# Batch 0 of k as fp32 over two hardware queues with a cast on chip, and a newly searched fixed order of all instructions

## Chip, cores, metric

One core of one Trainium2 chip. The metric is device time in microseconds (us) of one execution. Times are medians; comparisons use the runs in the fast state, taken on the same chip in the same rounds, with a 95% interval. A run counts as slow when it is over 1.5% above the fastest run of the same kernel.

## The reference, cut

```python
def phi(x):                                   # w_phi: 64 x 128
    proj = np.einsum('bhsd,df->bhsf', x, w_phi)
    proj = proj - np.max(np.abs(proj), axis=-1, keepdims=True)
    return np.concatenate([np.exp(proj), np.exp(-proj)], axis=-1)
q_p, k_p = phi(q), phi(k)                     # q, k, v: 8 x 8 x 576 x 64, fp32
kv  = np.einsum('bhsf,bhsd->bhfd', k_p, v)
num = np.einsum('bhsf,bhfd->bhsd', q_p, kv)
den = np.einsum('bhsf,bhf->bhs', q_p, np.sum(k_p, axis=2))[..., None] + 1e-06
x = (num / den)                               # then heads side by side: 4608 x 512
h = x @ w_in                                  # 512 x 2048
g = np.where(h > 0, h, np.exp(np.minimum(h, 0)) - 1)
out = g @ w_out                               # 2048 x 512
```

## The kernel before

The kernel is one long list of steps. One letter is one step of one kind, taken in turn from that kind's list of pieces; a star sends the step to the other of two engines, and a digit names a PSUM bank. Each engine executes its own instructions in the order in which the list has them. So the string below is the schedule.

```python
ORDER = """
eacdbeefgj7kfA0gj7BekBA2A4fCBj7hl6Bkl1hmBmA6gCBM0BCj3DBkENA4Dl3BEOmBP2l1EQCS2m*CFA0FTM6ECU4DTUNE
...                                           # 24 such lines
"""
for letter, star, bank in re.findall(r"([A-Za-z])(\*?)(\d?)", "".join(ORDER.split())):
    fn, args = queues[letter]
    ...
    fn(*next(args), **how)
```

The letters that matter here are: a start (w_phi, identity), b cast of w_phi, e/f/g loads of k/q/v, h/i loads of w_in/w_out, j/k transposes of k on TensorE and their copy, n/o DMA transposes of k and q, A k times w_phi, C its maximum, E v times its scale, S q times w_phi, x/R/y the division of the attention's result, z DMA transposes of that result into xT, p x @ w_in, q/r/s the ELU, t @ w_out. The prediction calls some steps by name: h_mm is p, q_mm S, m_mm M, x_mm W, v_scale E, h_elu s, x_scale y; kv_copy (V) and o_copy (u) copy products out of PSUM, the memory that TensorE writes to. Of the tiles, w_sb is the cast w_phi, mk the maxima of C, vs v times its scale em, and denj the denominator that R forms.

```python
def start():
    w_f32 = epool.tile([P, CHUNK], FP32, name="e_sb")[:, 0:F]
    for par in range(2):
        queue = (nc.sync, nc.scalar)[par]
        queue.dma_start(out=w_f32[par * D:(par + 1) * D, :], in_=w_phi)
    ...

def load(name, b, p0, p1):                    # e, f, g: fp32 in HBM, bf16 in SBUF
    nat = get((name, b), lambda: io.tile([P, H // 2, NS, D], BF16, name=name + "n"))
    nc.gpsimd.dma_start(out=nat[:, p0:p1]..., in_=src[b]...[:, p0:p1])

def v_scale(n, pr, sg):                       # E
    nc.gpsimd.tensor_tensor(get(("vs", n), new_vs)[:, sg, r, 0:D],
        st["v", n // 2][:, 2 * (n % 2) + pr],
        st["em", n][:, sg, r].unsqueeze(2).to_broadcast((P, NS, D)), op=ALU.mult)

def x_rec(n, part):                           # R: two inputs in SBUF (e1 and xs)
    den = small.tile([P, 7], FP32, name="denj")[:, 0:v1 - v0]
    nc.vector.scalar_tensor_tensor(
        den, st["e1", n][:, 0, v0:v1], 1e-6, st["xs", n, part][:, :, D],
        op0=ALU.mult, op1=ALU.add)
    nc.vector.reciprocal(st["rec", n, part], den)

def x_dma(n, pr, mixed):                      # z: xp (bf16) -> xT, read by h_mm (p)
    nc.sync.dma_start_transpose(out=xT_of(b)[:, ct]..., in_=xp...)
```

Of the kernel before, what the change touches and what calls it, by code (L numbers as in the profile page):

```python
# [10 lines left out]
FP32 = mybir.dt.float32  # L11
BF16 = mybir.dt.bfloat16
# [31 lines left out]


# [1 line left out]
def kernel(  # L47
# [26 lines left out]
    NS = S // D  # L74
# [10 lines left out]
    io = ctx.enter_context(tc.tile_pool(name="io", bufs=2))  # L85
# [4 lines left out]
    moep = ctx.enter_context(tc.tile_pool(name="moep", bufs=2))  # L90
# [115 lines left out]
    def load(name, b, p0, p1):  # L206
        src = {"k": k, "q": q, "v": v}[name]
        nat = get((name, b), lambda: io.tile([P, H // 2, NS, D], BF16, name=name + "n"))
        nc.gpsimd.dma_start(
            out=nat[:, p0:p1].rearrange("p r s d -> p r (s d)"),  # L210
            in_=src[b]
            .rearrange("h s d -> (h s d)")
            .rearrange("(pr q x) -> q pr x", q=P, x=NS * D)[:, p0:p1],
        )

    def load_w_in(j):
# [6 lines left out]
    def copy_on(scalar):  # L223
        return nc.scalar.copy if scalar else nc.vector.tensor_copy
# [504 lines left out]
    def blocks(name, n):  # L729
        cut = 3 if (name, n) == ("k", 0) else 5  # L730
        return [(name, n, 0, cut), (name, n, cut, NI)]
# [83 lines left out]
```

## Time and profile before

| | before |
|---|---|
| time, median of the three runs | 367.6 us (366.73 to 371.62) |
| span of the profiled run | 365.3 us |
| idle of TensorE between 60 and 361 us | 1.3 us of 301 |

TensorE is full from about 60 us on, and its clock is 0.9 or more of full speed in each of the page's 40 slices.

In the timeline a line is start, duration, queue or engine, source line, operation and operands. In this kernel xT lands 4.2 us after its issue.

### The profile page before, as it was taken

The numbers are of one execution on the slowest core, as the hardware profiler recorded it, in microseconds if no ns is written. First come the engines' busy times: TensorE is split into PE (matmuls) and PEld (weight loads), VectorE is DVE, ScalarE is ACT, GpSimd is POOL, SyncE is SP. The second block draws the span as 40 slices with busy tenths as digits, with TensorE's granted clock in tenths as the row PEclk, the third lists the DMA queues.
The fourth block names the chain that finished last, engine by engine and source line by source line (L and its number), as shares of the span: only waits on it lengthen the run. The fifth ranks groups of instructions, "written<-read, shape, count | busy, mean of one in ns | idle before, by whom it ended". The sixth has DMA issues, their size and how long they took to land.

```text
span 365.3 us, 9809 instructions
## 1 busy us (share of the span) xinstructions
PE 347.5 (95%) x3914; PEld 188.5 (52%) x3914; DVE 269.6 (74%) x476; ACT 251.8 (69%) x479; POOL 213.2 (58%) x323
## 2 busy tenths in 40 slices
PE   3788899999999999999999999999999999999994
PEld 2566676655465454545455445544555444444442
DVE  4899986878876889798978899899858814744300
ACT  4879788877897689877976886888577304554220
POOL 8673848277934988485776597556557404543200
PEclk9999999999999999999999999999999999999999
DMA  7999969599796999866989399053220330214143
GB/s 106 195 213 208 208 100 148 65 166 151 114 144 95 166 171 144 152 89 92 193 162 126 44 173 135 4 110 79 44 48 16 32 75 2 58 29 92 26 99 74
DMA packets 68478, 39.70 MB, mean 109 GB/s; under 512 B 48336, under 2 KB 62800, under 8 KB 68432
## 3 DMA queue, kind: packets, MB, share of 16 engines
q1 hardware_dynamic: 52416, 20.56, 33.1%
q0 software_dynamic: 15856, 18.35, 32.7%
q8 instruction: 30, 0.49, 0.6%
q14 instruction: 16, 0.13, 0.1%
q10 hardware_dynamic: 160, 0.16, 0.1%
HBM read 36.77 MB, written 9.44 MB: 126 GB/s over the span
## 4 chain that ended last, share of the span: by engine, by line
PE 77%; DVE 12%; DMA 7%; issue 1%; POOL 1%; ACT 0%; DVEq 0%; ACTq 0%; POOLq 0%
PE banks L693 32%; PE banks L665 29%; PE banks L509 4%; DMA kT<-kn 3%; DVE mk L305 3%; PE banks L542 3%; PE banks L469 2%; PE banks L287 2%; DVE gT L685 2%; DMA kn<-in_k_dram 2%; DMA qn<-in_q_dram 2%; PE banks L558 2%; DVE mq L388 2%; PE banks L346 2%; DVE xp L575 1%
## 5 line engine op out<-in xcount | busy, mean ns | idle before, releaser
L681 POOL TENSOR_SCALAR e_sb<-e_sb 128x512 f32<-128x512 f32 (+1 forms) x160 | 91.1, 574 | 96.2 <-ACT e_sb L676 93.1
L693 PE MATMUL banks<-w_out_sb,gT 128*128 128x512 bf16 x576 | 138.3, 380 | 0.0
L676 ACT ACTIVATE e_sb<-banks 128x512 f32<-128x512 f32 (+1 forms) x160 | 88.1, 561 | 62.1 <-PE banks L665 57.9
L685 DVE SCALAR_TENSOR_TENSOR gT<-e_sb,banks 128x512 bf16<-128x512 f32 (+1 forms) x160 | 97.0, 626 | 44.9 <-POOL e_sb L681 44.5
L665 PE MATMUL banks<-xT,w_in_sb 128*128 128x512 bf16 (+1 forms) x576 | 123.0, 356 | 1.1 <-DVE gT L685 0.3
L665 PEld LDWEIGHTS <-w_in_sb 128*128 128x128 bf16 x640 | 59.1, 98 | 58.9 <-issue 2.6
L298 ACT ACTIVATE EK<-banks 128x768 bf16<-128x768 f32 x96 | 75.7, 814 | 16.5 <-PE banks L287 14.5
L324 POOL TENSOR_TENSOR vs<-vn,em 128x576 bf16<-128x576 bf16 x64 | 73.6, 1159 | 17.8 <-ACT em L315 17.7
L693 PEld LDWEIGHTS <-gT 128*128 128x128 bf16 x576 | 52.3, 98 | 59.7 <-issue 1.9
L493 ACT ACTIVATE Eq<-banks 128x768 bf16<-128x768 f32 (+2 forms) x96 | 73.5, 813 | 6.9 <-PE banks L481 3.3
L305 DVE TENSOR_REDUCE mk<-banks 128x6 f32<-128x768 f32 x48 | 45.2, 950 | 6.2 <-ACT EK L298 3.9
L374 DVE TENSOR_REDUCE mx<-banks 128x6 f32<-128x768 f32 (+1 forms) x30 | 30.7, 1038 | 4.8 <-PE banks L346 3.8
L608 POOL TENSOR_TENSOR xj<-xs,recj 128x448 bf16<-128x448 f32 (+1 forms) x22 | 20.1, 916 | 13.9 <-DVE recj L603 10.6
L587 DVE TENSOR_TENSOR xs<-banks,e 128x455 f32<-128x455 f32 (+1 forms) x30 | 18.0, 602 | 7.4 <-PE banks L542 5.9
L703 ACT COPY o_sb<-banks 128x512 f32<-128x512 f32 x23 | 13.3, 589 | 14.5 <-PE banks L693 14.5
L509 PE MATMUL banks<-vs,EK 64*128 64x65 bf16 x1152 | 22.9, 192 | 0.2 <-DVE xp L575 0.2
L509 PEld LDWEIGHTS <-EK 64*128 64x128 bf16 x1152 | 20.9, 96 | 2.9 <-issue 1.3
L542 PEld LDWEIGHTS <-Eq 128*128 128x128 bf16 x400 | 16.2, 97 | 7.3 <-issue 1.3
L592 DVE TENSOR_TENSOR xs<-banks,xs 128x455 f32<-128x455 f32 (+1 forms) x30 | 18.3, 610 | 1.1
L287 PE MATMUL banks<-w_sb,kT 64*128 64x128 bf16 x288 | 17.1, 228 | 1.9 <-DVE kT L240 1.1
L542 PE MATMUL banks<-kv_sb,Eq 128*128 128x65 bf16 x400 | 17.2, 193 | 0.5 <-DVE kv_sb L519 0.5
L469 PE MATMUL banks<-qT,w_sb 64*128 64x384 bf16 (+2 forms) x102 | 16.4, 324 | 0.5 <-DVE gT L685 0.2
(66 smaller groups left out, 243.3 us busy)
## 6 DMA issues: line engine op xcount, KB each, us to landing
out_dram<-o_sb SPq DMA_DIRECT2D x71, 128.0 KB, 2.4
kn<-in_k_dram POOLq DMA_DIRECT2D x7, 576.0 KB, 9.2
qn<-in_q_dram POOLq DMA_DIRECT2D x7, 576.0 KB, 7.3
vn<-in_v_dram POOLq DMA_DIRECT2D x7, 576.0 KB, 8.6
w_in_sb<-in_moe_w_in_dram POOLq DMA_DIRECT2D x2, 1024.0 KB, 20.4
w_out_sb<-in_moe_w_out_dram POOLq DMA_DIRECT2D x1, 2048.0 KB, 20.4
qn<-in_q_dram POOLq DMA_DIRECT2D x2, 288.0 KB, 7.4
vn<-in_v_dram POOLq DMA_DIRECT2D x2, 288.0 KB, 8.1
```

The source lines that it names most:

```text
L298: nc.scalar.activation(EK[:, sg, 6 * c:6 * c + 6, :].rearrange("p (i r) f -> p r i f", r=2), st["pk", n, c], ACT.Exp, scale=1.0 - 2.0 * sg,)
L305: nc.vector.tensor_reduce(mk[:, 6 * c:6 * c + 6].rearrange("p (i r) -> p r i", r=2), st["pk", n, c], axis=AX.X, op=ALU.max, apply_absolute ...
L324: nc.gpsimd.tensor_tensor(get(("vs", n), new_vs)[:, sg, r, 0:D], st["v", n // 2][:, 2 * (n % 2) + pr], st["em", n][:, sg, r].unsqueeze(2). ...
L374: nc.vector.tensor_reduce(mq.rearrange("p (v r) -> p r v", r=2)[:, :, v0:v1], st["pm", n, c][:, :, 0:v1 - v0, :], axis=AX.X, op=ALU.max, a ...
L493: nc.scalar.activation(Eq[:, sg, :, :, p0 * D:p1 * D].rearrange("p h r x -> p r h x"), st["pq", n, c][:, :, 0:(p1 - p0) * P].rearrange("p ...
L509: nc.tensor.matmul(kv[:, hi, pr, sg, :], EK[rows, sg, pr * NS + s, :], vs[rows, sg, pr * NS + s, :], start=(s == 0), stop=(s == NS - 1),)
L542: nc.tensor.matmul(pn[:, sg, v - v0, :], Eq[:, sg, hi, par, i0 * D:(i0 + 2) * D], kv_sb[:, hi, pr, sg, :], start=True, stop=True,)
L665: nc.tensor.matmul(ph, w_in_sb[:, ct, jt * P:(jt + 1) * P], xT_of(ch)[:, ct, h0:h1], start=(ct == 0), stop=(ct == N_CT - 1),)
L676: nc.scalar.activation(e_sb, st["ph", ch, jt, h0], ACT.Exp)
L681: nc.gpsimd.tensor_scalar(e_sb, e_sb, 1.0, 0.0, op0=ALU.min, op1=ALU.max)
L685: nc.vector.scalar_tensor_tensor(gT[:, jt, h0:h1], st["e", ch, jt, h0], -1.0, st["ph", ch, jt, h0], op0=ALU.add, op1=ALU.max,)
L693: nc.tensor.matmul(po, st["gT", ch][:, jt, tt * P:(tt + 1) * P], w_out_sb[:, jt, :], start=(jt == 0), stop=(jt == N_JT - 1),)
```

## The change

The intent is to free the software queue (GpSimd's, over which all casting loads go) at the start: k of batch 0 comes as plain fp32 over SyncE's and ScalarE's queues, in four transfers of 288 KB, and VectorE casts it. v_scale may now go to VectorE, and the whole list was searched again with these freedoms. The counts of letters change little (14 of 64 v_scale to VectorE, four kv_copy to ScalarE, three o_copy and two x_scale to VectorE); the matmuls are the same 3914.

```diff
 ORDER = """
-eacdbeefgj7kfA0gj7BekBA2A4fCBj7hl6Bkl1hmBmA6gCBM0BCj3DBkENA4Dl3BEOmBP2l1EQCS2m*CFA0FTM6ECU4DTUNE
-...
+acdGj3kbA0BBfgfGj7kGA6A2GgefBBBCj5j1kA4BBBhhCkl0mCDDl0mA2BA0BBBCM6NOP5Q*l6l7m*CDS2TTCDmFFEEEEE*
+...                                          (24 lines, all new)
     def start():
+        k_f32 = moep.tile([P, H // 2, NS * D], FP32, name="gT")
+        nc.sync.dma_start(out=k_f32[:, 0], in_=k_src[:, 0])
         for par in range(2):
-            queue = (nc.sync, nc.scalar)[par]
-            queue.dma_start(out=w_f32[par * D:(par + 1) * D, :], in_=w_phi)
+            nc.scalar.dma_start(out=w_f32[par * D:(par + 1) * D, :], in_=w_phi)
+        nc.sync.dma_start(out=k_f32[:, 1], in_=k_src[:, 1])
+        nc.scalar.dma_start(out=k_f32[:, 2], in_=k_src[:, 2])
+        nc.sync.dma_start(out=k_f32[:, 3], in_=k_src[:, 3])
+    def k_cast(pr, other=False):              # G, on VectorE
+        copy_on(other)(nat[:, pr]..., st["k_f32"][:, pr])
-    def v_scale(n, pr, sg):
-        nc.gpsimd.tensor_tensor(
+    def v_scale(n, pr, sg, other=False):      # E* is VectorE
+        (nc.vector if other else nc.gpsimd).tensor_tensor(
-        e=(load, [("k", 0, 0, 1), ("k", 0, 1, 2), ("k", 0, 2, 4)]
-           + [("k", *x) for x in all_batches[1:]]),
+        e=(load, [("k", *x) for x in all_batches[1:]]),
+        G=(k_cast, [(pr,) for pr in range(H // 2)]),
```

More of the change, by code (lines that the diff above doesn't have):

```diff
@@ L18 @@
 ORDER = """
-eacdbeefgj7kfA0gj7BekBA2A4fCBj7hl6Bkl1hmBmA6gCBM0BCj3DBkENA4Dl3BEOmBP2l1EQCS2m*CFA0FTM6ECU4DTUNE
-BM2EOVDBNFW6EP5M0XM2Q*S4ENTU6FNOj1iP0UQ*kTS2VM0TNW4TY7OXS0j6Tl3kTY2mP5l4Z*W0mQ*Z*S3XA5Tp7j2qkTS0
-rCp2TM3TsNqp7BrA0sj4qCp3Brp2qsl6BkresM4qmp7BrNp3qM0qsrA4Drsp6Esp2qNl7Bp3rqp1O*sqrY0mrCZ*W6FEsp0B
-XP2gqp5Drp4qQqsrS6srqM2sFTsEM0NTp5rNqp7rS2qsM0sTrY6ENU4TsA0O*A2BUZp7VBp6qP5CBt4rsBS0p7TCtqQ*rW2T
-sp5DnXqW0qrtrXfp6ES2qsA0stBnrFsTp7Eu*t6TCp5qp4rDzqp3sqrp2Brszp7sqp5qrqS0rstrTsoFsEqp4Tp7rqzS2sA0
@@ L24 @@
-rTtEsCToU4qA2BUrzstV*CBW4up7XW0qBt6rXzDBM4FtNzM0M2sA4NvBp7tNqBzrA0sM2O*BCftBENP7t5uQCEDS2M6TtNFe
-TS0M6ETtNTEU2S0A6UTCop4VtqTp3rzBsW0qnp4Xrp2qszW0rqu*O*p3DXvBEp5qsvrp7qrszp6rqsFsA0rqM2np4NBEp5qC
-rzP3p2rQ*sqp3srqsDp7rqsfp6sqrBp5rsqEsM0qA2p4NBrt7BrsqFS0CgtTsrTS2EM5TNS0toTsTA5U2CTUBS0VvtBW2zTt
-6XTW4uzA0DXS2BtETzCtFETtzBA2M4BS0t7oTCtDTNFtEBvM0A4EM2NBtzNeBU0fu*UA2Cp6Bp5Cqut4rDBsEp7qM2V*rp6N
-qEDnW0wstwrqxgM2trNW0FnetxEp5vusS0qM2Rp7syTNp6TFrqS2Rp4qsrTrsp5qsTp7rqysW0qS2xp6rTzrTp4sEzsqA0U2
-qCroUrsBp7RV*syA5BCW2p4zxDqW0Eqxp3Brp2rBsRqA0S5qCnt7rTgRtsvTrstBEvsDS3M5TytNzTt2yu*BW3EzS5xA0tBF
@@ L30 @@
-zTRM3CtyTNFtzBEwM5S0vU3NTUToA5Vt7BuA0CtCzDtBEW2BtfxBA4p6BRyp3CqDEW0u*wp2qxrBp7FqFsrS0M4TEt6NTtrs
-qtRrsM0ysM3p5NEzp7qNp2rzqsW0rqp4nxrp5qevstrsqsrS0uU2RTUy*S6TzVp4TsW0vqp3xTrp5qoRrsA0qS6p2CTrp4Ts
-vqsW6qp3rzBrsp5qexBt2rqRS0DA6srotBsytBsyTA3CtETCzW5Dt7FxFBEtBnRM0yA5M3NBztEutNBzEM0wU2CvfUNDS4V*
-Et6uW0TvW2xTtxA4M0BntRBW2Nyzp7ECtqt1xFDrup5FsEA2qM6p4NBrp0ECqU6srBUqM2V*tNrA5sS2Bp7swRp4TRCyqp0T
-rztqsBtzrqgy*S2u*W5Torp7xDTp1sqS2qRvW5rsTp4rsTp0zyxqW2Fqp7zrsrsA5qvp1gRBxrp4qsBp3rsqyp2Cqrwzt7sq
-rsS0EM5sTtnNTrtEDzsS0M3A5TEtCoTt2NFBEA0U3BCURM5Dty*BEVztBNEW3zu*A0S5xBtTt7CTW3RDtxBEA5wM0Bu*FS3y
@@ L36 @@
-tNBEtTCp2TFuW0qU3xM5rURM0NV*p7yNp4zqsrS5qA0p3sTroCp2Tqsp7qrW4qrsp6DrsBnp3Rqsp2qrvxBt7rzqsA0S4srB
-tsBp6y*TCzp3qRp2qrvwtrsqzsDtrTEsvM0A3M5NBp2ENp1qBru*p0qEsvt7qCFrM5p2rsW3NqtrstFsExA0S5BtyTCt4TRW
-2By*txzDA0U5BRS2zUyBtEV*zCtuFDEvW0TS5xt7TEzTtu*ETS0U2TFS4UwTtVW0p6xp3qRTRW0rtqyTp2rxp5qsp4rqRW0r
-sqp6sursp3yqsp7qrzxp5rqy*zp4qrssW0rzqt6Rrsp3zxp7qy*W0rsqp2xrp5qstrsqtRrsp4systqzRp7rzst5qtrvsty*
-tzt7ztvttt4ttp3p2qp1rqstrqsp3rsp2qt1rqsp0rsp3qtrqsp2rsp0qu*p3rqvstrqsup6rvsp5qp3rqsp2rqsp6rqstrq
-st5rsp3p6qp2rqstrqsp3rsp6qutrqvsp7rsp3qp6rqstrqsup7rvst4qutrvstup7vp6qtrqst5rsp7u*p6qvtrqstrstt7
@@ L42 @@
-p6p4qtrqsp3rstqtrsp6t4qutruvstvtt7utvttt6tutvtt7u*tvttuv
+acdGj3kbA0BBfgfGj7kGA6A2GgefBBBCj5j1kA4BBBhhCkl0mCDDl0mA2BA0BBBCM6NOP5Q*l6l7m*CDS2TTCDmFFEEEEE*
+M4U6NOUM0NV*W6XP4Q*S2TTM0M4NNEEFFU6EUV*OP0QS2TTM0NW5XY4S0TTj7j3j2kkkY5Z*ZgiOP6Q*W0XS3TTA5l2mCS0T
+TM3Nl2mA0CBBp7qp3qrrl4msBj5kp2qp4srM6NBqrsp5qrssY1DZ*M6NA2Bp4qp5p1qqrrrCDsssW6Xp0p4Bqqp5ql1m*p2
+p3p6FFrrrsqqrsp7qsqY4M0sO*P5Q*Z*p2qrrrsssS5TTNM3M0NNp7qS3TTEEE*ErU5sA0CfrsUV*A2p6BBO*P4p7p5eQ*S0
+ot4tqqrrqTTCBrsssBDW6XzEW0Xnzttu*p6qrp7qrsS2TTA0Cp5qp4qt6Bgsrp2qp3qrrssBsp7rFqrDp5qFrssp4qS0TTS2
@@ new lines @@
+otp7tE*E*rEssnqrsTTA0CU4fUV*A2Ctu*BBDEBBW4p7qrW0XXt6M2NtM0sA4BM2NNzzzzvzzp7qrstA0FBBBCDM2NtO*P7
+Q*t5uCS2TTM6NtS0TM6NEEFU3EUVetS2oTTTA6CDW0XBE*E*tuBp3qrFp4qrW1Xp6p7p0qssrsqrsqp5p6rsqqrsO*p7M2N
+A0Bqp5p4qqznnvp2CBrsrrssqp3qp7rfsrsDqp6qrrssp5qgrFrM0NA2BP7Q*Bp4S0qTTEsCst7tS2TM5NS0TTTtrsA5CBB
+U2EUtS0wTTVW2XW4t6S2DEEA0CuttTTzzzovvzzXvzzDtu*A2BBBM4CS0ot7ttTTBM0M2NNNA4BBtuegFFeU0EEUV*A2nnCD
+CFEEp7qrW0xRy*p4qt5W0p6tDsxBBrqsrsttuM3M1S6TTp0qwp5E*NNEFM3Np7qqp6qp4frrssRrsqS0TTW2p5qp7qrsxrs
+A0vvCS2TTorsp6qRrsyzrsp4qrsU2UV*A5CyW2xRBBDBp7qBW0xp4p3p2rqqqrssrrssA0nvRCE*S5t7tS2TTwM5NzTTttu*
@@ new lines @@
+t3DW4BA6BBBEE*yyxRFyFzzzzzzvCS1TTotttM4M6uNNS1TTt0U3EUA1A6CCtV*W3DFxRttE*u*BBBBA3BBW1xCp5p6gep0q
+qqp1qt4p7ttrsRy*rfrrqrssssS0DFTTM2NM5Ntup7qW2xM0Np6p4p5yEEEqwrrvvnS0zzqrqsssU2US6TTTp4TqVW0p3wrR
+syzovxqp5S6rrsRsqrA0p2p4TTqrCDBqssW6xp3p5rsqrgsBqt2A6CnS0oTTztW3tA0rsFRCyxBBDBBtt7tM0u*RA5M3NNtt
+M0EEFyzzEU2BBCDuEUV*S4TNwTyEEzt6W0W2xRyxRettM0A4Btp7BNvzvCnyzquW2xp0p4qqrrrM5A2BDt1tssNFFEsBp0qC
+M6NU4S2TTErUVtA5CsRS3ToTp7DE*qrp2W3sxRyy*BqtuBvp0p7p1qrrW5ssqqp4qrrfsgS2TTxp0qp7A5rssW2xBp1p4qq
+p3BEqrrrrsssRCsqrp2qDt7M0NS5srsTTttS0TTnA5CM3Nzztt2A0CEEFFu*U3UBBM5NRyy*tDV*wW3xtBEBA5BCS0TTtW3x
@@ new lines @@
+uBRt7tFDEEA3S0TTCoM5NBBzzzvzp2tqW0tuy*vvxRRU3M5FEUV*M0NNp7p3qqS5oTTznrrssA0Cyzp2qrrssp4p7p6p3qqr
+rssW4wxp2t7BqrsDBqS4FqrsrsA0TBp6p3BE*E*yqp2qqCttrrsrssTzzzM0NRM5NA3tu*BBvp2qrp0qrp5qrp7qrssCst6t
+sS2TTA0M4NCttW3xRt7tBBuS0TA5DDE*y*yBBTwCDW2xRttu*t4tS5FFEU0UTTS2TTttvuVW0W6t5FEEEtyxRxRS2TTU0EU
+V*W6zzztW0W3wy*xRyy*xxRp2p6tp1p7qrqrzzqqrssrp2p6p0qqzvvzvRsu*yy*W4p1srsqp3rsrsqrqsp7p6p2qqqxrrss
+rRrzzzy*zzp0qrp3qsp4qssrrssp6t5ttp3qrqp2qrrstp1qt7tssrsp0p2qrtp1tp4p3p6qqqsqu*ursrsrsrsqrst1tp3
+p0tqrqp4qp2qrrrsssp5qtt6tttrsst5p7p2qp0qqrvvuvrrsssp3p4ttqqrrssp7qrp0tp4qqu*u*st3tp1p2qqrsrrrp0q
@@ L43 @@
+p7ttvsu*sst5tttt3tttvuvvp4p2vqrrqssp7rsqqrp0p1p6qsrsqqrsrt5ttrsstuut6tvvttu*t7ttvtu*t4tttuvv
 """
@@ L171, in start @@
         w_f32 = epool.tile([P, CHUNK], FP32, name="e_sb")[:, 0:F]
-        for par in range(2):
-            queue = (nc.sync, nc.scalar)[par]
-            queue.dma_start(out=w_f32[par * D:(par + 1) * D, :], in_=w_phi)
-        st["w_f32"] = w_f32
+        k_f32 = moep.tile([P, H // 2, NS * D], FP32, name="gT")
+        k_src = k[0].rearrange("h s d -> (h s d)").rearrange(
+            "(pr q x) -> q pr x", q=P, x=NS * D
+        )
+        nc.sync.dma_start(out=k_f32[:, 0], in_=k_src[:, 0])
+        for par in range(2):
+            nc.scalar.dma_start(out=w_f32[par * D:(par + 1) * D, :], in_=w_phi)
+        nc.sync.dma_start(out=k_f32[:, 1], in_=k_src[:, 1])
+        nc.scalar.dma_start(out=k_f32[:, 2], in_=k_src[:, 2])
+        nc.sync.dma_start(out=k_f32[:, 3], in_=k_src[:, 3])
+        st["w_f32"], st["k_f32"] = w_f32, k_f32
         for j in range(2):
@@ L213, in load @@
             .rearrange("(pr q x) -> q pr x", q=P, x=NS * D)[:, p0:p1],
+        )
+    def k_cast(pr, other=False):
+        nat = get(("k", 0), lambda: io.tile([P, H // 2, NS, D], BF16, name="kn"))
+        copy_on(other)(
+            nat[:, pr].rearrange("p s d -> p (s d)"), st["k_f32"][:, pr]
         )
```

## The prediction

> **What bounds the kernel now.** I read the page's busy shares first, then busy time by stage, then the chain of waits for the pace of a matmul, and last the timeline of the start, because the change touches the start and the order of everything else.
>
> ```profile
> PE 347.5 (95%) x3914; PEld 188.5 (52%) x3914; DVE 269.6 (74%) x476; ACT 251.8 (69%) x479; POOL 213.2 (58%) x323
> ...
> 0.00:40.00 40.00, 28.79 (x506) 22.43 (x507) 31.87 (x65) 29.50 (x59) 26.46 (x47) 1.00 1.08 183
> 40.00:60.00 20.00, 18.98 (x292) 13.52 (x289) 17.26 (x39) 16.86 (x38) 13.25 (x25) 1.00 0.87 139
> 60.00:361.00 301.00, 299.73 (x3125) 152.52 (x3122) 220.46 (x375) 204.98 (x384) 173.47 (x252) 1.00 0.60 97
> ...
> 277.94 4.32 PE banks L665 x20
> 346.96 13.83 PE banks L693 x64
> 102.40 1.15 PE banks L509 x72
> ```
>
> The columns of the stage rows are the stretch, its length, busy time of PE, PEld, DVE, ACT and POOL, then clock, DMA share and GB/s. TensorE is the bound, at full clock (1.00). But a busy TensorE is not one at full pace. The chain gives the pace: 20 matmuls of 512 columns in 4.32 us and 64 in 13.83 us are 216 ns each; 72 of 64 rows and 65 columns in 1.15 us are 16 ns each. Scaling these by columns (half the time for 64-row matmuls, which run two at a time), I estimate the work at full pace. 1088 of 512 columns at 216 ns are 235.0 us; 128 of 256 at 108 ns are 13.8; 1152 of L509 at 16 ns are 18.4; 640 of 65 columns (L542, L558) at some 31 ns are 19.8; 704 of 64 rows x 128 columns at 27 ns are 19.0; the 102 wide ones of L469 7.7; 100 full transposes and small ones at 54 ns 5.4. The sum is 319 us. The span of 365.3 us therefore holds about 46 us that are not matmul work: 4.5 us after the last matmul (347.0 + 13.8 = 360.8), and, counting the matmuls of each line that ran before 60 us (107 of L665, 20 of L693, 216 of L509 and so on: 35.4 us at full pace), 24.6 us in the first 60 us, and 301 - 283.6 = 17.4 us in the other 301 us. The first 60 us are 16% of the span and hold more than half of the loss.
>
> ```profile
> 1.24 0.75 POOL L209 DMA_DIRECT2D kn<-in_k_dram  x1 [0.79 <-POOLq L799]
> 2.54 1.28 POOL L209 DMA_DIRECT2D kn<-in_k_dram  x2
> 3.80 0.72 POOL L209 DMA_DIRECT2D qn<-in_q_dram  x1
> 4.56 0.50 PE L233 MATMUL banks<-ident,kn 128*128 128x128 bf16 x3 [4.56 <-DMA kn<-in_k_dram]
> 6.69 0.71 PE L233 MATMUL banks<-ident,kn 128*128 128x128 bf16 x5 [0.45 <-DMA kn<-in_k_dram]
> 7.44 0.56 DVE L240 COPY kT<-banks 128x768 bf16<-128x768 bf16 x1 [1.98 <-PE banks L233]
> 10.45 1.14 PE L233 MATMUL banks<-ident,qn 128*128 128x128 bf16 x9 [0.92 <-DMA qn<-in_q_dram]
> ...
> 15.00:20.00 5.00, 4.36 (x110) 3.71 (x110) 4.93 (x9) 4.16 (x8) 4.54 (x7) 1.00 1.22 212
> 30.00:35.00 5.00, 4.40 (x52) 3.34 (x51) 5.00 (x9) 5.00 (x11) 1.36 (x4) 1.00 1.22 207
> 40.00:50.00 10.00, 8.98 (x179) 6.66 (x175) 9.71 (x22) 8.86 (x19) 7.31 (x14) 1.00 1.19 193
> ...
> q0 software_dynamic: 7936, 9.50, 95.5%
> ```
>
> The reader should see three different limits in the start. Until 12 us the kernel waits for k and q: the first matmul starts at 4.56 us, the second part of k arrives at 6.69, q at about 10.4. From 12 to 50 us VectorE is nearly full (4.93 of 5, 5.00 of 5, 9.71 of 10). And the last row, the DMA view of the first 60 us, has the software queue holding 95.5% of the DMA engines, so w_in (issued at 8.1 and 8.8 us, landed 18 to 22 us later) cannot come much sooner; the first h_mm starts at 29.8 us.
>
> **What the Trainium skill says.** (1) "DMA: Bandwidth & Descriptors", section SWDGE vs HWDGE vs iDMA: a cast during DMA is possible only from GpSimd, so an fp32 transfer over SyncE or ScalarE needs a cast on chip; the kernel before agrees in form, all its casting loads are on POOL's queue. (2) The same page, "Issuing engines are not separate DMA queues": all queues share the same 16 engines, and more issuing engines save only issue time. The 95.5% agrees that bandwidth, not the number of queues, is short from then on. (3) "VectorE: DVE Perf Modes", the perf-mode tier table: a copy between SBUF tiles from fp32 runs at twice the elements per cycle, `tensor_tensor` with an fp32 input at one, with the formula (N+151)/0.96. The trace agrees with the latter: the DVE row of L608 with 448 elements has 620 ns, the formula 624. No row before has the large cast. (4) "GPSIMD Engine Reference", When to use GPSIMD: two-input operations are about twice as slow there. Here vs on POOL takes 1159 ns for 576 elements; the formula gives an estimated 757 ns on VectorE.
>
> **The change part by part.**
> Removed: three casting issues of k from POOL, 0.75 + 1.28 = 2.03 us of its time. POOL then makes the identity at once, so `sel_small` and `sel` (1.35 us on VectorE) can begin about 0.7 us sooner, and q is issued at about 1.9 us in place of 3.80.
> Added: four plain loads of 288 KB, the first issued at 0.74 us as w_phi was. w_phi (32 KB) landed by 2.95; k's first quarter should be in by about 3 to 3.3 us. Then the cast. Four casts of 128x576 on VectorE, an estimated (288+151)/0.96 = 0.46 us each, 1.8 us in all. The first stands behind `sel` in VectorE's order, so it starts at some 3.5 us, ends at 4.0, and the first transpose starts near 4.1 in place of 4.56: only 0.4 us sooner. The second part of k gains more, about 1.2 us (VectorE now waits 1.98 us for it), and q about 2 us. Both w_phi halves now go over ScalarE's queue, the second behind the first by one issue (0.58 us); w_sb's cast stands behind the first kT copy now, so that hides.
> HBM bytes do not change; k's SBUF writes double (1.2 MB for 0.6), which I take as hidden[...].
> Head, summed: VectorE is idle 8.1 us of the first 40. Earlier k and q can remove perhaps 4 us of that; 1.8 us goes to the casts and 0.75 us to one v_scale that now runs there early, while two kv_copy (0.7 us each) leave for ScalarE. Net 4.0 - 1.8 - 0.75 + 1.4 = 2.9, less some 0.7 for waits that take their place: I expect 2.2 us sooner at the 50 us mark, and that shift carries to the end because TensorE is the bound after it.
> The new order: counted over the whole order list, 14 of 64 v_scale move to VectorE (+14 x 0.757 = 10.6 us there, -16.2 us on POOL), 4 more kv_copy go to ScalarE (-2.8 on VectorE, +2.4 on ACT), 3 more o_copy to VectorE (+2.0), 2 more x_scale (+1.3), two qT/mT copies and others near nothing. VectorE with the casts: 269.6 + 10.6 - 2.8 + 2.0 + 1.3 + 1.8, about 282 us (77%); POOL about 193. That lies beside TensorE, which keeps the same 3914 matmuls, unless VectorE gets tight between 120 and 240 us, where it is busy 35 of 40 us already. What the order can win is the 17.4 us of steady loss. I counted, in TensorE's order, how much matmul work stands between the writing of a PSUM bank and its next use: for h_mm the median goes from 3.7 to 3.95 us, for m_mm 2.06 to 2.18, for x_mm 1.9 to 2.6, for q_mm 2.6 to 2.4. Slightly more slack, so I give it 10% of the loss, 1.8 us.
> Sum: 367.6 - 2.2 - 1.8 = 363.6 us.
>
> **Rivals.**
> (a) The start is bound by w_in and VectorE, not by k. Then the earlier k only lets VectorE wait later: 0 to 1 us. For: the full DMA engines and VectorE rows above, and casts plus one v_scale put on the very engine that is full. Against: the DMA engines are not full before about 12 us (58 and 103 GB/s in early slices of the first 60 us, 208 later), which fp32 loads can fill. Total about 366.
> (b) VectorE becomes the bound in the middle: 12 us more work on an engine at 88% there, and h_elu waits. For: VectorE already has several of the chain's links (mk 3.0%, gT 2.2%). Against: the moved work frees POOL, which h_elu waits for now (44.5 us in the waits view), and a search chose it. Total 368 to 371.
> (c) The search found much more than I can see from slack: half of the 17.4 us and 4 us of the start. For: the order has new freedom and was searched as a whole. Against: the order before was searched too. Total 355 to 358.
>
> **Range and chances.** Twice the head's plausible error (2 us) and the order's (from +3 to -6) give 358.5 to 367.5 us. Faster by over 2% means below 360.2 us, which needs most of (c): 0.22. Slower by over 2% (above 375) needs (b) at more than I can derive: 0.02. Same: 0.76.
>
> **What would show it.** Head: first transposes at 3.9 to 4.3 us, q's at 8 to 9, casts at 0.4 to 0.5 us each, first h_mm at 27 to 29. Idle of VectorE in the first 40 us near 5 us. Order: PE loss after 60 us of some 15.6 us, L324 on DVE 14 times at about 0.76 us, VectorE about 282 us. I am wrong if the first h_mm starts as late as before (rival a), if PE waits for DVE grow in the middle (b), or if the loss after 60 us falls below 12 us (c).

## More of the kernel before

Busy time by stage, for two stretches that will matter (stretch, length, then busy us of PE, PEld, DVE, ACT and POOL with the numbers of instructions, then clock, DMA share and GB/s):

```profile
110.00:130.00 20.00, 20.00 (x233) 10.00 (x233) 16.32 (x25) 14.72 (x33) 14.31 (x20) 1.00 1.01 138
165.00:185.00 20.00, 20.00 (x222) 10.10 (x220) 18.04 (x34) 17.55 (x31) 13.51 (x21) 1.00 0.98 157
```

The chain of waits already runs through DMA for 7% of the span. And the timeline around 110 us shows why the transposes of xT cost TensorE nothing here: the last of them is issued five microseconds before the next casting loads.

```profile
109.45 1.21 SPq L649 DMA_TRANSPOSE xT<-xp  x1
...
114.52 0.83 POOL L209 DMA_DIRECT2D kn<-in_k_dram  x1
```

## The result, and the profile after

The changed kernel takes 383.32 us (378.23 to 385.47 in four runs, one of them, 385.47, slow), beside 369.37 for the kernel before in the same rounds. The ratio is 1.035 [1.025, 1.045]: slower by 3.5%, where 1.1% faster was predicted. All ratios here are those of fast runs of one kernel over fast runs of the kernel before in the same rounds; they are not quite the ratio of the medians. The profiled span is 381.1 us, 15.8 more than before.

The page of the changed kernel: busy time, TensorE's two rows of slices, and the chain by engine.

```profile
PE 350.2 (92%) x3914; PEld 189.4 (50%) x3914; DVE 285.9 (75%) x491; ACT 253.4 (66%) x484; POOL 198.4 (52%) x304
...
PE   2698989999996999997989999999999999999995
...
PEclk9999999999999899998999999999999999999999
...
PE 62%; DVE 17%; DMA 12%; issue 3%; ACT 3%; POOL 2%; ACTq 0%; DVEq 0%; POOLq 0%
```

TensorE has holes where it had none, in the 13th and 19th slices (about 114 to 124 and 171 to 181 us), and the granted clock is lower in the 14th and the 19th. DMA's share of the chain is 12%, from 7%. The same stretches by stage:

```profile
110.00:130.00 20.00, 15.80 (x194) 8.13 (x191) 12.27 (x19) 11.80 (x24) 10.36 (x14) 0.91 1.13 167
165.00:185.00 20.00, 17.48 (x185) 8.42 (x184) 14.39 (x25) 11.38 (x22) 11.12 (x16) 0.91 1.08 159
```

All five engines do less than before, VectorE too, and only the DMA share is higher: nothing computes because something has not arrived.

To place the loss I counted the weight loads of each line by a time t and multiplied them by the full-pace times that the prediction gives. This is work done in us, an estimate from the traces (rows e3, e5 and e8 are experiments told below). A recount with the prediction's rounded times comes out 1.2 to 2.8 us lower throughout, and within 0.3 us of the row of differences:

| work done by | 60 | 120 | 140 | 160 | 180 | 200 | 300 us |
|---|---|---|---|---|---|---|---|
| before | 37.1 | 93.0 | 111.2 | 129.2 | 147.7 | 166.3 | 260.6 |
| after | 34.7 | 90.4 | 103.7 | 120.5 | 135.3 | 152.8 | 245.2 |
| after behind | 2.4 | 2.6 | 7.5 | 8.7 | 12.4 | 13.5 | 15.4 |
| e3 | 34.7 | 90.1 | 107.4 | 122.4 | 141.0 | 157.8 | 252.1 |
| e5 | 34.5 | 89.9 | 106.9 | 125.3 | 144.2 | 163.0 | 257.2 |
| e8 | 34.1 | 90.3 | 104.1 | 121.8 | 134.7 | 151.9 | 244.9 |

So 2.4 us are lost in the head, where 2.2 were to be won; 4.9 between 120 and 140; 3.7 between 160 and 180; and the rest in small pieces.

**The hole at 120 us.** The timeline of the changed kernel:

```profile
111.85 0.83 POOL L216 DMA_DIRECT2D kn<-in_k_dram  x1
112.68 0.75 POOL L216 DMA_DIRECT2D vn<-in_v_dram  x1
113.69 0.74 POOL L216 DMA_DIRECT2D kn<-in_k_dram  x1
113.98 1.60 SPq L662 DMA_TRANSPOSE xT<-xp  x1
...
124.35 0.38 PE L678 MATMUL banks<-xT,w_in_sb 128*128 128x512 bf16 x1 [4.20 <-DMA xT<-xp]
```

Three casting loads of 576 KB of bf16 each now stand just ahead of the transpose of xT. The bracket says that TensorE was idle 4.20 us until xT landed. In the chain of waits the transfer itself is one piece (start, length, what):

```profile
113.98 10.33 DMA xT<-xp
...
165.70 10.59 DMA qT<-qn
```

The transpose took 10.33 us for 4.2 before. The second line is the same at 165.7 us with the transpose of q, beside loads issued at 163.69 and 164.51; TensorE then waits 1.58 and 0.94 us for it and is nearly idle from 173 to 176. After each hole the clock falls, as single microseconds by stage show (same columns as above):

```profile
123.00:124.00 1.00, 0.00 (x0) 0.00 (x0) 0.00 (x0) 0.00 (x0) 0.00 (x0) 1.00 1.29 202
...
125.00:126.00 1.00, 1.00 (x9) 0.45 (x7) 0.59 (x1) 0.42 (x1) 0.49 (x1) 0.50 1.23 209
...
128.00:129.00 1.00, 1.00 (x17) 0.69 (x16) 0.40 (x1) 1.00 (x2) 0.40 (x1) 0.86 2.96 215
```

In 123 to 124 no engine does anything, and the DMA share is 1.29. Then TensorE is granted half its clock for some 3.4 us: "busy" again, at half the pace. The Trainium skill, "TensorE: Matmul & The Clock Gate", Part 1: The HAM clock gate, says that after an idle window of about 3.4 us the clock goes to 1.2 GHz and comes back after about as long of sustained work. This trace agrees: 4.20 us idle, then 0.50 for about 3.4 us, a further 1.7 us of work lost.

**The stall at 200 us.** The timeline of the changed kernel:

```profile
195.67 2.25 POOL L337 TENSOR_TENSOR vs<-vn,em 128x576 bf16<-128x576 bf16 x2
195.78 2.17 DVE L612 SCALAR_TENSOR_TENSOR denj<-e,xs 128x7 f32<-128x7 f32 x1
...
200.62 0.40 PE L359 MATMUL banks<-w_sb,qT 64*128 64x128 bf16 x8 [1.67 <-ACT EK L311]
```

An addition of 7 numbers per partition on VectorE takes 2.17 us, and ends when two v_scale on GpSimd end. TensorE, some steps further on, waits 1.67 us. The view of the tile denj gives the same operation's durations (count, then ns minimum, median and maximum). Before:

```profile
L599 DVE SCALAR_TENSOR_TENSOR denj<-e,xs x30: 119/164/539, 126.1 to 290.2; 128x7 f32<-128x7 f32 x20, 128x6 f32<-128x6 f32 x10
```

After:

```profile
L612 DVE SCALAR_TENSOR_TENSOR denj<-e,xs x30: 118/170/2168, 126.7 to 304.2; 128x7 f32<-128x7 f32 x20, 128x6 f32<-128x6 f32 x10
```

The median is the same; only the worst case grew, from 0.54 to 2.17 us. The Trainium skill, "SBUF — State Buffer", section SBUF: two separate sides, says that VectorE and GpSimd share a pair of ports as an exclusive lock, and that a VectorE operation with two SBUF inputs is fully blocked while a GpSimd operation that reads SBUF holds it. That fits this line, and the experiments test it.

**The head.** The timeline of the changed kernel:

```profile
1.98 0.60 ACTq L180 DMA_DIRECT2D gT<-in_k_dram  x1
...
9.58 0.83 DVE L225 CAST kn<-gT 128x576 bf16<-128x576 f32 x2 [2.29 <-DMA gT<-in_k_dram]
10.32 0.95 DVE L318 TENSOR_REDUCE mk<-banks 128x6 f32<-128x768 f32 x1
12.28 0.71 PE L246 MATMUL banks<-ident,qn 128*128 128x128 bf16 x5
```

The first transpose of k starts at 4.32 us, 0.24 sooner than before. But k's part on ScalarE's queue, issued at 1.98, lands at 9.56, beside the loads of q and v, issued from 1.46 on (e7 below shows that these hold it up); VectorE, executing in order, waits 2.29 us for it with the casts ahead of the first maximum of k, which starts at 10.32 (before: 7.92). The first h_mm starts at 34.33 us, before at 29.81. How much of this is the new path and how much the new order, e1 and e2 tell.

### The profile page after: what moved, and what is told of

The parts are those of the page before. It is cut to its first block, busy times and chain, and to the rows that moved or that the text cites. A ratio compares the mean times of both kernels' runs of the same rounds, so it can differ in the third digit from the quotient of the medians.

```text
span 381.1 us, 9834 instructions
## 1 busy us (share of the span) xinstructions
PE 350.2 (92%) x3914; PEld 189.4 (50%) x3914; DVE 285.9 (75%) x491; ACT 253.4 (66%) x484; POOL 198.4 (52%) x304
## 4 chain that ended last, share of the span: by engine, by line
PE 62%; DVE 17%; DMA 12%; issue 3%; ACT 3%; POOL 2%; ACTq 0%; DVEq 0%; POOLq 0%
PE banks L706 26%; PE banks L678 21%; DVE gT L698 5%; PE banks L522 3%; DMA qT<-qn 3%; DMA xT<-xp 3%; DMA kn<-in_k_dram 2%; PE banks L555 2%; DMA kT<-kn 2%; DMA gT<-in_k_dram 2%; PE banks L300 2%; PE banks L482 2%; PE banks L571 2%; POOL e_sb L694 2%; DVE xs L600 1%
## 5 line engine op out<-in xcount | busy, mean ns | idle before, releaser
L694 POOL TENSOR_SCALAR e_sb<-e_sb 128x512 f32<-128x512 f32 (+1 forms) x160 | 92.5, 585 | 114.6 <-ACT e_sb L689 111.3
L678 PEld LDWEIGHTS <-w_in_sb 128*128 128x128 bf16 x640 | 60.1, 98 | 60.8 <-issue 4.8
L311 ACT ACTIVATE EK<-banks 128x768 bf16<-128x768 f32 x96 | 74.2, 817 | 13.6 <-PE banks L300 10.5
L506 ACT ACTIVATE Eq<-banks 128x768 bf16<-128x768 f32 (+2 forms) x96 | 72.7, 816 | 13.4 <-PE banks L482 8.7
L337 POOL TENSOR_TENSOR vs<-vn,em 128x576 bf16<-128x576 bf16 x50 | 58.0, 1175 | 20.4 <-ACT em L328 17.6
L716 ACT COPY o_sb<-banks 128x512 f32<-128x512 f32 x20 | 11.8, 591 | 23.5 <-PE banks L706 21.0
L621 POOL TENSOR_TENSOR xj<-xs,recj 128x448 bf16<-128x448 f32 (+1 forms) x20 | 18.3, 918 | 14.1 <-DVE recj L616 14.0
L716 DVE COPY o_sb<-banks 128x512 f32<-128x512 f32 x16 | 11.0, 685 | 14.8 <-PE banks L706 14.8
L555 PEld LDWEIGHTS <-Eq 128*128 128x128 bf16 x400 | 15.8, 98 | 11.7 <-issue 7.1
```

The costliest lines, as they stand in the source:

```text
L311: nc.scalar.activation(EK[:, sg, 6 * c:6 * c + 6, :].rearrange("p (i r) f -> p r i f", r=2), st["pk", n, c], ACT.Exp, scale=1.0 - 2.0 * sg,)
L337: (nc.vector if other else nc.gpsimd).tensor_tensor(get(("vs", n), new_vs)[:, sg, r, 0:D], st["v", n // 2][:, 2 * (n % 2) + pr], st["em", ...
L506: nc.scalar.activation(Eq[:, sg, :, :, p0 * D:p1 * D].rearrange("p h r x -> p r h x"), st["pq", n, c][:, :, 0:(p1 - p0) * P].rearrange("p ...
L555: nc.tensor.matmul(pn[:, sg, v - v0, :], Eq[:, sg, hi, par, i0 * D:(i0 + 2) * D], kv_sb[:, hi, pr, sg, :], start=True, stop=True,)
L678: nc.tensor.matmul(ph, w_in_sb[:, ct, jt * P:(jt + 1) * P], xT_of(ch)[:, ct, h0:h1], start=(ct == 0), stop=(ct == N_CT - 1),)
L694: nc.gpsimd.tensor_scalar(e_sb, e_sb, 1.0, 0.0, op0=ALU.min, op1=ALU.max)
```

## The experiments

The theories to be told apart: (1) the new path of k costs; (2) the order costs, by loads standing ahead of transposes; (3) VectorE has become the bound through the 14 v_scale; (4) two-input VectorE operations wait on GpSimd's port. All outputs are right.

**e1: before's order, new path of k.** The old list with its first three loads of k removed and the four casts put where k is needed.

```diff
-eacdbeefgj7kfA0gj7BekBA2A4fCBj7hl6Bkl1h...
+acdfgGj7kbfA0gGj7BekBA2A4fCBGGj7hl6Bkl1h...
```

> The order of the kernel before, with batch 0 of k as fp32 over the SyncE and ScalarE queues and four casts on VectorE put in where k is first needed. Theory A (the new order is what costs, by loads bunched against DMA transposes; the new k path costs about 2 us in the head): ratio to before 1.000 to 1.008, no TensorE stall over 1 us after 60 us. Rival B (the new k path is what costs): ratio 1.03 or more.

Measured: 1.001 [0.998, 1.004], 367.21 us. In the old order the new path wins nothing and loses nothing: theory 1 falls. In the head the gains are spent again: k's first product is at 6.16 us (before 5.52), since w_sb's cast waits for the second half of w_phi, now second on ScalarE's queue; TensorE waits 1.32 us there. The first h_mm starts at 30.0 us, and by a recount of the work done e1 stands only 0.2 us behind the kernel before at 60 us.

**e2: new order, old path of k.** The new list without G and with three e again; start and loads as before.

```diff
-acdGj3kbA0BBfgfGj7kGA6A2Gg...
+eacdbeej3kA0BBfgfj7kA6A2ge...                 (three e again, no G)
```

> The new order with k of batch 0 loaded by casting DMAs from GpSimd as before (three issues first in GpSimd's order, no casts on chip). Theory A: still slow, ratio 1.02 to 1.035, with TensorE stalls of some microseconds behind DMA transposes between 110 and 200 us and half clock after them. Rival B: ratio about 1.00.

Measured: 1.031 [1.027, 1.036], 378.24 us. Nearly the whole loss is in the order. e1 and e2 together settle which half of the change to look into. They also split the head. With the old path of k the new order still starts h_mm late, and by the recount it is 1.3 us behind at 60 us, where the changed kernel is 2.4 behind:

```profile
L671 PE MATMUL banks<-xT,w_in_sb x96: 269/272/283, 33.3 to 59.3; 128*128 128x256 bf16 x96
```

The last times are those of the first and the last start: 33.3 us for the first h_mm, 29.81 before, 34.33 in the changed kernel.

**e3: five casting loads later in the new order.** The loads of v of batch 4, k and q of batch 5, v of 5 and of 7 are moved behind the transposes near them. Nothing else moves.

```diff
-...A4BBtuegFFeU0EE...rsrsttuM3...p7qqp6qp4frrss...orsp6qRrs...p6gep0q...rrfsgS2TT...
+...A4BBtueFFU0EE...rsrstgtuM3...p7eqqp6qp4rrss...orsp6fqRrs...p6ep0q...rrfsS2TT...   (v of 5, 7 later on)
```

> The changed kernel with five load issues moved later in GpSimd's order, well ahead of their first use still: v of batch 4, k and q of batch 5 (two of them stand beside k of batch 4 within 2.6 us), v of batch 5 and v of batch 7. Nothing else changes. Theory A: the stall of 4.2 us at 120 us and the half clock after it go, 5 to 6 us; the stall at 173 us shrinks too, so 5 to 10 us of the 14 come back: ratio 1.008 to 1.022. If the order is slow for another reason (VectorE overloaded): ratio stays above 1.03.

Measured: 1.024 [1.021, 1.028], 376.02 us, just over the forecast of 1.008 to 1.022 and about 1% better than the changed kernel, though the two intervals overlap. The hole at 120 goes, xT lands in 6.82 us, but two new stalls open, of 2.09 us at 141 and 1.65 us at 195. The timeline of e3 around the first:

```profile
137.12 0.62 POOL L694 TENSOR_SCALAR e_sb<-e_sb 128x512 f32<-128x512 f32 x1
137.46 2.36 DVE L612 SCALAR_TENSOR_TENSOR denj<-e,xs 128x6 f32<-128x6 f32 x1
137.71 0.94 POOL L621 TENSOR_TENSOR xj<-xs,recj 128x448 bf16<-128x448 f32 x1
138.62 1.18 POOL L694 TENSOR_SCALAR e_sb<-e_sb 128x512 f32<-128x512 f32 x2
...
141.26 0.40 PE L300 MATMUL banks<-w_sb,kT 64*128 64x128 bf16 x5 [2.09 <-DVE gT L698]
```

VectorE is held not by one GpSimd instruction but by four in a row, from 137.46 to 139.82: the last ends at 139.80. TensorE then waits for VectorE, and its clock is at half from 141.4 to 144.8. In the changed kernel this collision did not happen at this place. We take it that such a collision depends on how the two engines stand to each other at that moment, which every shift changes; no run tests this.

**e4: all v_scale back to GpSimd.**

```diff
-...FFEEEEE*M4U6...        +...FFEEEEEEM4U6...     (all 14 E* become E)
```

> The changed kernel with its 14 v_scale of VectorE put back on GpSimd. Rival C (VectorE with 10 us more work bounds the middle): ratio falls from 1.035 to below 1.02. Theory A: ratio 1.03 to 1.045, since the stalls come from DMA transposes, and GpSimd issues its loads no earlier.

Measured: 1.058 [1.056, 1.061], 388.3 us, above both forecasts. If VectorE had become the bound, taking 14 x 0.84 us from it should have helped; it got worse (1.058 against 1.035 for the changed kernel). Alone this does not settle it, since GpSimd got 14 operations of 1.15 us more, and TensorE's waits for qT rose from 2.5 to 5.2 us. What settles it are e5 and e13 below: they keep all 14 on VectorE and end at 1.006 and 1.007, and in e13 VectorE has 11% of the chain, for 12% before. Theory 3 falls.

**e5: e3, and denj with one SBUF input.** The 1e-6 is dropped on purpose, so that the operation has one input; it is the same size.

```diff
-        nc.vector.scalar_tensor_tensor(
-            den, st["e1", n][:, 0, v0:v1], 1e-6, st["xs", n, part][:, :, D],
-            op0=ALU.mult, op1=ALU.add)
+        nc.vector.tensor_reduce(
+            den, st["xs", n, part][:, :, D:D + 1], axis=AX.X, op=ALU.max)
```

> On top of the spread loads: the tiny denominator step of the joined groups (denj, which reads two SBUF tensors and took up to 2.36 us instead of 0.16 while GpSimd ran) becomes a reduce over one element of one SBUF tensor, so it drops the 1e-6 of the denominator (a relative change under 1e-6). Theory D (a VectorE operation with two SBUF inputs waits until GpSimd's queue of work pauses, and holds up the PSUM banks behind it): the stalls of 2.09 us at 141 us and 1.65 us at 195 us shrink to under 0.7 us, no half clock at 141, ratio from 1.024 to 1.008 to 1.016. Rival (the long durations are only where VectorE would have waited anyway): ratio stays 1.020 or more.

Measured: 1.006 [1.001, 1.012], 369.86 us, a little better than forecast. With both mended, 3.5% of loss are down to 0.6%. The view of the tile in e5:

```profile
L612 DVE TENSOR_REDUCE denj<-xs x30: 113/157/167, 123.2 to 292.5; 128x7 f32<-128x7 f32 x20, 128x6 f32<-128x6 f32 x10
```

None of 30 takes over 0.167 us. In the timelines of the changed kernel and of e5 alike, 11 of the 30 start while GpSimd is at work and stays so for over 0.16 us more; in the changed kernel 10 of these 11 take 0.27 to 2.17 us, in e5 none is longer than the others. And xT is issued at the same time as in the changed kernel (114.10 and 113.98 us), but lands after 6.79 us in place of 10.33: the transpose was not simply issued late. Last, the first stage with a DMA hole, by stage in e5 (TensorE is busy 19.12 us again, and the clock is full; from 165 to 185 it is 19.58):

```profile
110.00:130.00 20.00, 19.12 (x229) 9.91 (x233) 16.68 (x25) 15.34 (x31) 13.59 (x17) 1.00 0.94 164
```

**e8: one SBUF input alone, loads as in the changed kernel.** The edit is that of e5, without the moves of e3.

```diff
-        nc.vector.scalar_tensor_tensor(den, ..., 1e-6, ...)
+        nc.vector.tensor_reduce(den, ...)
```

> The changed kernel as it was (loads bunched) with only the one-input denj. Theory D with A: the stalls behind xT at 120 us and qT at 173 us stay, the one at 199 us goes; gain 1.5 to 4 us, ratio 1.024 to 1.031. If D is wrong: 1.035.

Measured: 1.039 [1.034, 1.045], 382.23 us. A gain to 1.024 to 1.031 was expected, and this missed: alone the edit wins nothing. Its timeline shows where that went:

```profile
175.71 0.45 PE L359 MATMUL banks<-w_sb,qT 64*128 64x128 bf16 x10 [3.70 <-DMA qT<-qn]
```

The wait for qT grew from 1.58 + 0.94 to 3.70 + 1.92 us and the half clock after it lasts 7 us (176 to 183). What arrives late makes time saved before it worthless.

**e12: one SBUF input in before's order**, as a control on e1 (edit as in e5).

```diff
-        nc.vector.scalar_tensor_tensor(den, ..., 1e-6, ...)     # in e1
+        nc.vector.tensor_reduce(den, ...)
```

> Control for the one-input denj: the old order with the new k path, where denj never took over 0.54 us. Theory D (the step matters only where it meets a busy GpSimd): ratio 0.998 to 1.001, as e1. Rival (the step is simply cheaper, anywhere): 0.990 to 0.996.

Measured: 1.002 [0.999, 1.006], 368.05 us. The one-input form is not faster in itself. What e5 won over e3 is the collisions.

**e10: before, with its loads bunched.** The loads of v of batch 4 and k of batch 5 are moved directly behind that of k of batch 4.

```diff
 (before's list)  -...e(k4)...g(v4)...e(k5)...    +...e(k4)g(v4)e(k5)...
```

> The kernel before (old order, old k path) with v of batch 4 and k of batch 5 issued directly behind k of batch 4, as the new order has them; nothing else. Theory A (loads in a bunch hold up the DMA transposes issued behind them): the kT transposes issued near 122 us land 3 to 6 us later, TensorE waits 2 to 5 us for one of them, a half clock of some 3.4 us may follow: ratio 1.006 to 1.018. Rival (bunching is harmless, the new order's transposes are simply late): ratio 0.998 to 1.003.

Measured: 1.001 [0.998, 1.004], 367.68 us: no effect. A loss was expected from theory 2, and this missed. The timeline of e10:

```profile
110.14 1.22 SPq L649 DMA_TRANSPOSE xT<-xp  x1
...
115.29 0.83 POOL L209 DMA_DIRECT2D kn<-in_k_dram  x1
...
116.86 0.76 POOL L209 DMA_DIRECT2D kn<-in_k_dram  x1
```

The bunch is as tight as in the changed kernel, but xT was issued five microseconds ahead. The transposes of k issued behind the bunch took 9.8 to 10.9 us, and nobody needed them yet. In the kernel before itself, which issues two loads just beside them, the same two took 12.9 us each, and TensorE waited 0.8 us. So theory 2 has to be narrower: loads must stand ahead of a transpose, and that transpose must be needed soon.

**e13: a bunch kept, but behind the transposes** (new order, one input). v of batch 4, k and q of batch 5 together some 10 us later; v of batch 5 and 7 moved too.

```diff
-...A4BBtuegFFeU0EE...p7qqp6qp4frrss...
+...A4BBtueFFU0EE...p7egqqp6qp4rfrrss...
```

> The new order with one-input denj, where k of batch 5, v of batch 4 and q of batch 5 are issued in a bunch as tight as the one that stalls, but some 10 us later, behind the xT and qT transposes; v of batch 5 likewise between k 6 and q 6. If what counts is loads AHEAD of an urgent transpose: as e5, ratio 1.003 to 1.011, no stall over 1.5 us. If the bunch itself counts: stalls move to the next transposes, ratio 1.018 or more.

Measured: 1.007 [1.002, 1.013], 369.4 us, the same as e5 within the intervals. A bunch behind the transposes costs nothing that these runs can see; the first wait for xT is down to 0.98 us:

```profile
120.66 0.38 PE L677 MATMUL banks<-xT,w_in_sb 128*128 128x512 bf16 x1 [0.98 <-DMA xT<-xp]
...
127.09 0.83 POOL L216 DMA_DIRECT2D kn<-in_k_dram  x1
```

**e14: only the first bunch put back** (e5, with v of batch 4, k and q of batch 5 at the changed kernel's places).

```diff
-...A4BBtueFFU0EE...rsrstgtuM3...p7eqqp6...orsp6fqRrs...       (as e5)
+...A4BBtuegFFeU0EE...rsrsttuM3...p7qqp6...p4frrss...
```

> e5 with v of batch 4, k and q of batch 5 back at their places of the new order (ahead of the xT transpose at 114 us), the later loads still spread. If the loads ahead of xT cause the stall at 120 us: that stall of 3.5 us or so and the half clock behind it are back, the one at 175 us is not; ratio 1.017 to 1.026, between e5 (1.006) and e8 (1.039). If the two stalls are not separable: about 1.039 or about 1.006.

Measured: 1.022 [1.017, 1.026], 375.34 us. The stall and the half clock (125.5 to 129) are back, and at 175 us there is none:

```profile
114.80 0.74 POOL L216 DMA_DIRECT2D kn<-in_k_dram  x1
...
124.76 0.38 PE L677 MATMUL banks<-xT,w_in_sb 128*128 128x512 bf16 x1 [3.50 <-DMA xT<-xp]
```

Against e5 this one bunch is worth 1.6% of the kernel before (1.0218 - 1.0063), some 5.7 us, which is more than the stall of 3.50 and the 1.7 of the half clock by 0.5.

**The head: e6, e7, e9, e11.** e6 is e5 with the third and fourth cast behind the first maximum of k. e7 is e1 with w_sb's cast on GpSimd ahead of its loads. e9 is e1 with the two halves of w_phi first, one on each queue, and k alternating behind them. e11 is e6 with e9's loads.

```diff
 e6   -acdGj3kbA0BBfgfGj7kGA6A2GgefBBBC     +acdGj3kbA0BBfgfGj7kA6A2gefBBBCGG
 e7   -nc.vector.tensor_copy(w_sb, ...)      +nc.gpsimd.tensor_copy(w_sb, ...)   (and b ahead of the first f)
 e9, e11   +for par in range(2): (nc.sync, nc.scalar)[par].dma_start(out=w_f32[...], in_=w_phi)
           +then k parts 0 and 2 on nc.sync, 1 and 3 on nc.scalar
```

> e5 with the third and fourth cast of k behind the first mk reduce in VectorE's order (they wait for a load that lands at 9.6 us, and the reduce waits behind them). Theory: VectorE's idle of 2.3 us before 9.6 us is used, the first banks come free earlier, and the head gains 0.5 to 1.5 us against e5: ratio 0.002 to 0.004 below e5. Rival (the head is bound by VectorE and the w_in load later on): no difference from e5.

Measured: 1.004 [0.998, 1.010], 369.38 us.

> The old order with the new k path (ratio 1.0008), with the w_sb cast put on GpSimd ahead of its first load, so that GpSimd issues q only at some 4.5 us and the fp32 loads of k have the DMA engines alone. Theory (k's second half lands at 9.4 us because it shares the engines with q and v): it lands by 6.5 us, q by 9 us, ratio 0.993 to 0.999. Rival (the start is bound later by VectorE or w_in): ratio 1.000 to 1.005, since w_in is issued 3 us later.

Measured: 0.998 [0.993, 1.003], 367.01 us. GpSimd issues its first load at 6.35 us here, and the last two parts of k land 5.0 and 5.1 us after their issue, beside 7.4 and 6.7 in e1: it was the loads of GpSimd that held them up. The time does not tell of it.

> The old order with the new k path, with the two halves of w_phi first on SyncE and ScalarE again and the four k loads behind them, alternating. In e1 the first k matmul waited 1.3 us for w_sb, whose second w_phi half came late; here it should start by 5.4 us in place of 6.16, and the start gains 0.5 to 1 us: ratio 0.996 to 1.000. Rival: the start is bound later (VectorE, w_in), ratio 1.000 to 1.002.

Measured: 1.003 [0.999, 1.007], 368.27 us.

> The new order with spread loads, one-input denj, later casts (e6, 1.0038) and w_phi first as in e9. If the late w_sb is what is left of the head: ratio 0.999 to 1.003. If not: as e6.

Measured: 1.004 [1.001, 1.008], 368.7 us. None of the four is told from its neighbour by the interval, so no gain that was forecast for the head is shown. By the estimate of work done, the head of the new order comes back in part (by 60 us: changed kernel 34.7, e6 35.0, e11 35.7, before 37.1). No kernel is faster than the one before beyond the noise.

## Why the prediction was wrong

**Kept: the parts.** The casts take 456 ns each (predicted 0.46 us). The formula behind it stands in another section of its page than the tier table, and there for fp32 `tensor_tensor`; to use it with half the elements for a cast was the prediction's own step. The first transpose starts at 4.32 us (3.9 to 4.3). VectorE is busy 285.9 us (282), POOL 198.4 (193). v_scale on VectorE has a median of 752 ns (757), though its mean is 836 and its worst 1399. It was right that what is won or lost in the head carries on (2.4 us behind at 60 us, 2.6 at 120), and that 14 v_scale do not make VectorE the bound: e5 and e13 show that against rival (b), which had named the right direction of the time with the wrong cause.

**Failed, the larger step: "Slightly more slack, so I give it 10% of the loss, 1.8 us."** The order was judged by one kind of wait, the reuse of PSUM banks, and got a gain from it. What the order changed is two other things. It put three casting loads ahead of a transpose that TensorE needed some 6 us later, which cost 4.20 us of idle time and the half clock after it, and it did nearly the same at 165 us. And it let a two-input VectorE operation meet longer runs of GpSimd work. e2 puts 3.1% of the 3.5% on the order; e5, with both mended, leaves 0.6%. The Trainium skill page that the prediction cites for one set of 16 DMA engines under all queues ("DMA: Bandwidth & Descriptors", Issuing engines are not separate DMA queues) already held the first, but the prediction used it for the head alone and never asked what stands in front of each transpose, although the order's list shows that.

**Failed, the smaller step: "I expect 2.2 us sooner at the 50 us mark".** It came out 2.4 us later by 60 us. The term "Earlier k and q can remove perhaps 4 us of that" failed: VectorE's idle in the first 40 us was to fall from 8.1 to about 5 us and is 8.7, and q's first transpose, forecast at 8 to 9 us, starts at 12.28. Part of it is the new path: k's part on ScalarE's queue landed 7.58 us after its issue, because q's and v's loads, issued sooner, share the DMA engines with it (e7), and two casts stood ahead of the first maximum. Against rival (a)'s row the prediction argued that the DMA engines had room before 12 us; at 185 GB/s in the first 10 us (109 before) they filled that room with transfers that were not the next ones needed. But in the old order the same path costs 0.2 us by 60 us (e1), and moving the two casts in the new one brings back about 0.5 (e6 against e5). By the same estimate the larger part, 1.3 of the 2.4 us, comes with the new order alone (e2), which the sum for the head holds only as work moved between engines. What in the order costs it is not isolated.

**The sizes do not add up one by one.** The first bunch is worth 1.6% (e14 against e5), the two-input operation 1.8% (e5 against e3) once the loads are spread, but nothing before (e8): behind a late transfer a saved wait is waited again. Spreading the loads alone brought 1.1% (e3), since new collisions came up; with the one-input operation in place it brings 3.3% (e8 to e5).

**Open.** Some 0.4% of the mended new order (e11) is not explained; it looks like the head by the work done, but no run isolates it, nor what in the new order costs 1.3 us there. Why the transposes wait for loads issued ahead of them, over another queue, is seen in the times only. That two-input operations wait for GpSimd's hold on the ports fits the page and the durations; the runs show the wait, not the lock. That the half clock at 176 us in e8 is longer than in the changed kernel is read from one profile each.

## What to carry to other kernels

In a fixed order, look for each DMA that a busy engine will need within some 10 us, and count the bytes issued ahead of it on any queue: the number of instructions and the slack of buffers don't show this. A gap of TensorE can cost more than itself: here one of 2.09 us and one of 4.20 each cost half of the next 3.4 us as well, one of 1.67 did not. And give small VectorE operations on the critical path one SBUF input where GpSimd is busy; when such a fix brings nothing alone, test it again with the other waits mended.

## What the Trainium skill lacked or had wrong

- "DMA: Bandwidth & Descriptors": no section gives how long a DMA transpose takes beside casting loads from GpSimd. Here 10.33 us behind three loads of 576 KB, 4.2 when issued five microseconds ahead of them, 9.8 to 10.9 in e10, and 12.9 for the transposes of k in the kernel before. Its section Issuing engines are not separate DMA queues agrees with the runs: loads from GpSimd's queue delay transposes from SyncE's.
- "SBUF — State Buffer", SBUF: two separate sides, says that the winner holds the port pair for the whole instruction. In e3 the VectorE operation waited 2.36 us across four GpSimd instructions in a row, the longest of them 0.94 us. A reader would take one instruction as the worst case; it is a whole run of them.
- "TensorE: Matmul & The Clock Gate", Part 1: The HAM clock gate, names an idle window of about 3.4 us. The return agrees (0.50 for some 3.4 us), but a shorter gap was enough here: 2.09 us idle in e3, and 1.58 and 0.94 us in close succession in the changed kernel. After 1.67 us at 200 us the clock stayed full.
- "GPSIMD Engine Reference", When to use GPSIMD, has two-input operations about twice as slow on GpSimd. v_scale measures 1154 ns there and 752 on VectorE (medians in the changed kernel), 1.5 times. The page names VectorE's 2x mode as one reason for its figure; em is fp32 here, and 752 ns are what its one-element formula gives, so that mode plays no part.
- "VectorE: DVE Perf Modes", the perf-mode tier table, held for the cast: 456 ns against an estimated 0.46 us.
